# Fp16 products for three late pieces of a spectral filter, and a new order around one register load

## The chip, the cores and the metric

The kernel runs on one core of a Trainium2 chip. The metric is the device time of one execution in microseconds (us). The core has five engines with an instruction stream each: TensorE (PE, matrix products; its weight loads are shown as PEld), VectorE (DVE), ScalarE (ACT), GpSimd (POOL) and SyncE (SP). SP and POOL mostly issue DMA transfers here. Engines wait for each other through semaphores, and each works through its own stream in program order.

## The reference

Two independent computations stand side by side in one output of 2048 x 896. The left half is attention with 16 query heads of 28 dimensions and one shared key and value head; the right half is a spectral filter: a two-dimensional real FFT of a 2048 x 448 array, a product with a complex filter, and the inverse FFT.

```python
q = (x @ wq).reshape(B, S, H, Dh).transpose(0, 2, 1, 3)      # H = 16, Dh = 28
k, v = x @ wk, x @ wv
scores = einsum("bhqd,bkd->bhqk", q, k) * Dh ** -0.5
o = einsum("bhqk,bkd->bhqd", softmax(scores), v)
a = o.transpose(0, 2, 1, 3).reshape(B, S, H * Dh) @ wo

X = rfft2(x2, axes=(-2, -1)) * (w_r + 1j * w_i)
b = irfft2(X, (S, D), axes=(-2, -1))
return concatenate([a, b], axis=-1)
```

## The kernel before

The kernel has a prologue and one long attention loop.

**Prologue.** A small planner (`Plan`) takes tasks with an engine, an estimated length and dependences, and writes each engine's instruction order; TensorE's tasks keep the order in which they are added. The prologue projects queries, keys and values in split precision (L340), transforms the first pieces of the filter's input, and prepares the values for the loop: 16 transposes (L606) put the values with the positions on the partitions into one PSUM bank. They stand in two halves, `first_values` and `last_values`. `last_values` begins with `values_load`, which reads one number (`bits`) into a register of every engine. A branch on that register (L646) follows; its body, a fallback for large scores, isn't executed with these inputs. After the branch VectorE copies the turned values to SBUF (`vs`, L718), and writes the low parts of the second half of the keys (`keys_low(1)`), which two DMAs then double (`keys_twice`).

**The attention loop.** There are 4 query blocks x 4 head groups = 16 groups of 16 steps (one step is 128 key positions). A step is two score pairs (`scores`, L1258: 8 fp16 matmuls of 512 columns into two PSUM banks, then one exponential of 128 x 1024 on ScalarE, L1261) and one value group (`values`, L1277: four fp32 matmuls of 512 columns, each issued as two instructions). Six banks hold scores, three pairs in turn; nine tiles hold exponentials.

**Fillers.** Banks 6 and 7 are left. One collects the values of the group at hand, the other is free for a filler: a unit of TensorE work for something else, followed by an eviction on VectorE that frees the bank. The loop is written out ahead of time by a schedule with three clocks (`clk`): `after(when, ...)` puts VectorE's work, and DMA issues, at planned times, and `fill` puts units between steps. `owed` grows by a fixed amount per step (`EARLY`: 0.22 us until the first half of piece 7 is copied out, then 0.13 us) until the filter's last stage is open (`fb`), and from then on by what is left over the steps that are left; a unit may be placed where `owed` is above 0, outside the first step and the last two steps of a group. Unit kinds are `l` (late pieces), `w` (output projection, L1196), `z` (the filter's last stages, L1094 and L1120).

**The late pieces.** The filter's first stage runs over eight pieces q of its input. Pieces 0 to 3 are done in the prologue. Piece 4 has its features in the prologue and its points in the loop; pieces 5, 6 and 7 lie wholly in the loop. For each:

- `late_load` brings its input x (512 KB) and its point matrix w (256 KB) on SP's queue. Pieces 5 and 6 are loaded in the prologue, piece 7 behind piece 6's work.
- `late_fold` adds and subtracts mirrored rows on VectorE, in three parts.
- `late_features(q, p)`, p = 0 and 1, is TensorE's transform along the feature axis (L173, fp32, 16 matmuls of 113 columns, issued as 32 instructions), planned at 0.86 us; VectorE copies the result out (L1013).
- `late_points(q, p)` is the first transform along the position axis (L1026, fp32, 8 matmuls of 226 columns, issued as 16 instructions), planned at 0.76 us; VectorE copies it out (L1035), and SP stores it (`fft1_store`).

After piece 7, `spectrum` starts the rest of the filter on VectorE: maxima are brought together by `bounce` (write 128 x 2 numbers to DRAM, read them back to every partition, reduce), the pieces are read again across partitions (`spread`, L802, on POOL), and butterflies with the filter product in their middle follow (L817 to L939). `weight_top` takes maxima of the eight filter weight blocks ahead of that (L893), from a planned time of 24 us on. The scales of the filter's last stage come from these maxima.

## Time and profile before

| what | us |
|---|---|
| time, median of 3 runs | 579.97 |
| lowest and highest | 579.77, 580.02 |
| the profiled execution's own time | 579.57 |
| its span | 577.8 |
| TensorE busy | 571.3 |
| ScalarE busy | 513.3 |
| VectorE busy | 390.5 |
| GpSimd busy | 110.5 |

The span is the time from the first to the last instruction in the trace; the time of an execution is a little longer. A busy share is an average over stages with different limits, and matmuls overlap in their pipeline, so a TensorE that is 99% busy isn't one at its peak. In rows of instructions in order of time the columns are start, length, engine, line, operation, output and inputs, count, and in brackets the idle time before it with what ended it. Instructions that follow each other closely are merged into one row.

### The profile page before, as it was taken

The page shows a single profiled execution, that of the slowest core. Times are in us where ns is not written, and L with a number is a line of the kernel's source. Part 1 is how long each engine was busy: PE and PEld are TensorE (multiplying, and loading weights), DVE is VectorE, ACT ScalarE, POOL GpSimd, SP SyncE. Part 2 cuts the span into 40 slices and gives each one's busy share as a digit, 9 for nine tenths or more (in the row PEclk, how much of TensorE's full clock was granted, in tenths as well). Part 3 has the DMA queues.
Part 4 walks back from the last instruction along what each step waited for, and adds up shares of the span by engine and source line. Part 5 has one row for each costly group of instructions (what it writes and reads, how often), then busy time and mean ns, then how long its engine had stood idle before and what let it go on. Part 6 is the DMA issues. An engine that isn't in the chain of part 4 may idle for free.

```text
span 577.8 us, 20635 instructions
## 1 busy us (share of the span) xinstructions
PE 571.3 (99%) x8941; PEld 300.6 (52%) x8941; DVE 390.5 (68%) x747; ACT 513.3 (89%) x580; POOL 110.5 (19%) x199
## 2 busy tenths in 40 slices
PE   9999999999999999999999999999999999999997
PEld 7877454545554444444444444445455555555554
DVE  5996727955421999998998887854366743366544
ACT  4744899999999999999999999998999887899982
POOL 1023311212103012121201311123202321011110
PEclk9999999999999999999999999999999999999999
DMA  8864682625417102243301120457224341212111
GB/s 290 295 205 140 175 247 73 191 81 146 161 37 218 58 18 66 75 123 98 91 34 57 41 60 31 155 208 230 78 88 128 109 130 70 89 58 73 41 55 65
DMA packets 38502, 66.27 MB, mean 115 GB/s; under 512 B 7013, under 2 KB 28653, under 8 KB 38401
## 3 DMA queue, kind: packets, MB, share of 16 engines
q1 hardware_dynamic: 29576, 38.95, 21.1%
q0 software_dynamic: 8688, 25.76, 14.2%
q8 instruction: 70, 1.15, 0.8%
q14 instruction: 24, 0.19, 0.1%
q10 hardware_dynamic: 144, 0.23, 0.1%
HBM read 44.22 MB, written 19.97 MB: 111 GB/s over the span
## 4 chain that ended last, share of the span: by engine, by line
PE 72%; issue 7%; DVE 5%; DMA 3%; POOL 2%; ACT 0%; POOLq 0%; DVEq 0%; ACTq 0%
PE banks L1258 31%; PE banks L1277 30%; PE banks L1196 6%; PE banks L1094 2%; PE banks L1120 2%; DMA rd<-rs 1%; DMA wf<-w 1%; DVE X L817 1%; DVE X L818 1%; PE banks L1026 1%; POOL R L1164 1%; DVE X L859 1%; PE banks L173 0%; ACT yb L1208 0%; DVE w L852 0%
## 5 line engine op out<-in xcount | busy, mean ns | idle before, releaser
L1261 ACT ACTIVATE p<-banks 128x1024 f32<-128x1024 f32 x512 | 477.2, 1094 | 23.7 <-PE banks L1258 22.3
L1258 PE MATMUL banks<-qa,ka 128*32 128x512 f16 x4096 | 276.4, 379 | 0.4 <-PEq L646 0.4
L1277 PE MATMUL banks<-p,vs 128*32 128x512 f32 x2048 | 268.6, 592 | 0.0
L1258 PEld LDWEIGHTS <-ka 128*32 128x32 f16 x4096 | 129.5, 96 | 167.1 <-issue 119.1
L1277 PEld LDWEIGHTS banks<-p,vs 128*32 128x32 f32 x2048 | 69.9, 110 | 43.5 <-issue 1.7
L1156 POOL DMA_DIRECT2D sd<-qraw x15 | 10.1, 671 | 165.4 <-DVE qraw L1151 165.4
L1196 PE MATMUL banks<-woh,o 128*32 128x448 f16 x464 | 39.6, 353 | 0.1
L1164 POOL DMA_DIRECT2D R<-rd x60 | 30.8, 521 | 38.3 <-DMA rd<-rs 38.1
L1196 PEld LDWEIGHTS <-o 128*32 128x32 f16 x720 | 22.6, 97 | 27.4 <-issue 20.2
L859 DVE SCALAR_TENSOR_TENSOR X<-w,X 128x226 f32<-128x226 f32 (+2 forms) x72 | 34.1, 474 | 2.4
L1151 DVE TENSOR_SCALAR qraw<-banks,scales 128x512 f32<-128x512 f32 x15 | 11.3, 750 | 31.5 <-PE banks L1277 31.4
L1201 DVE TENSOR_SCALAR ya<-banks,scales 128x448 f32<-128x448 f32 x12 | 8.2, 683 | 27.5 <-PE banks L1196 27.5
L1127 DVE TENSOR_SCALAR w<-banks,scales 128x256 f32<-128x256 f32 x16 | 7.7, 484 | 27.3 <-PE banks L1120 27.3
L1162 POOL DMA_DIRECT2D rd<-rs x15 | 8.2, 549 | 90.1 <-DVE rs L1161 81.6
L1196 PE MATMUL banks<-wol,o 128*32 128x448 f16 x256 | 24.4, 352 | 0.0
L340 PE MATMUL banks<-xh,wqh 128*128 128x512 f32 x64 | 23.6, 399 | 0.0
L340 PE MATMUL banks<-xh,wql 128*128 128x512 f32 x64 | 23.0, 390 | 0.0
L344 ACT ACTIVATE qraw<-banks 128x512 f32<-128x512 f32 x16 | 9.3, 595 | 15.0 <-PE banks L340 15.0
L817 DVE TENSOR_TENSOR X<-X 128x904 f32<-128x904 f32 (+2 forms) x10 | 9.1, 906 | 16.1 <-DMA X<-t 16.1
L852 DVE SCALAR_TENSOR_TENSOR w<-X 128x113 f32<-128x113 f32 (+2 forms) x56 | 17.8, 356 | 0.1
L1035 DVE COPY bs<-banks 128x452 f32<-128x452 f32 x8 | 5.0, 619 | 18.6 <-PE banks L1026 18.5
L340 PE MATMUL banks<-xl,wqh 128*128 128x512 f32 x48 | 17.3, 390 | 0.0
(157 smaller groups left out, 553.1 us busy)
## 6 DMA issues: line engine op xcount, KB each, us to landing
qa<-qd SPq DMA_DIRECT2D x62, 128.0 KB
ob<-yo SPq DMA_DIRECT2D x16, 256.0 KB
t<-bs SPq DMA_DIRECT2D x16, 226.0 KB
w<-w POOLq DMA_DIRECT2D x8, 452.0 KB, 4.7
X<-t POOLq DMA_DIRECT2D x8, 452.0 KB, 7.1
wf<-w POOLq DMA_DIRECT2D x8, 452.0 KB, 4.0
x<-t POOLq DMA_DIRECT2D x8, 452.0 KB, 4.4
R<-rd POOLq DMA_DIRECT2D x60, 56.0 KB, 2.1
```

Of the source, the lines that this page charges most:

```text
L340: mm(pq[c, g], w[:, j, gs], x[:, j], start=(j == 0 and n == 0), stop=(j == 3 and n == 1))
L817: todo(226 * n, lambda: TT(both(a), both(a), both(b), op=ALU.add), at)
L852: STT(out, y, sy, x, op0=ALU.mult, op1=ALU.add if c > 0 else ALU.subtract)
L859: todo(226 * n, lambda d=d, q=q: STT(both(d), t[0].rearrange("p r n f -> p r (n f)"), q, both(a), op0=ALU.mult, op1=ALU.add))
L1094: mm(pz[r, j], fb["c2", q % 2][:, x, e, j, r], fb["fi", q % 2][:, j, f], start=(n == 0), stop=(n == 2))
L1120: mm(py[m:m + 32, k].rearrange("p (j n) -> p j n", j=4), cs3[:w, kind, f, m:m + 32], fb["z", q % 2, e][:w, x, :, 64 * r:64 * r + 64], star ...
L1151: V.tensor_scalar(o, bank[b], scale_v, None, op0=ALU.mult)
L1164: nc.gpsimd.dma_start(R[32 * i:32 * i + DH], rd[i:i + 1].to_broadcast([DH, CW]))
L1196: mm(p[r:r + 32], x[c][:, g, s][:, r:r + 32], w[:, m], start=(g == 0 and n == 0), stop=(g == NG - 1 and n == 2))
L1258: mm(bank[b + h][r], ka[:, k:k + 32], qa[c, g][:, 2 * p + h], start=True, stop=True)
L1261: nc.scalar.activation(pt[i], banks[:, b:b + 2], AF.Exp, scale=SCALE / UP / UP)
L1277: mm(bank[b][32 * i:32 * i + 32], vs[:, kc], pt[2 * st + i // 2][:, i % 2], start=(kc == 0), stop=(kc == 15))
```

## The change

Three things are changed.

1. **Fp16 products for pieces 5, 6 and 7.** Features and points of these pieces are each computed from three fp16 products (high x high, high x low, low x high) in place of one fp32 product. The constants come split into two fp16 halves, scaled by 1024. The folded input is scaled by a number taken from its maximum and split on VectorE (`late_split`, two instructions per piece), the features are split when they are copied out (two instructions in place of one), and the points' copy multiplies the scales back. The maxima of the three inputs are taken early in the loop (`late_top`) and brought together by `bounce`, now for three columns. Piece 4 stays in fp32. Piece 7's loads move to the start of the loop, in buffers of their own, and the fp16 cosines are loaded there, where the fp32 ones were.
2. **The order around the register load.** All 16 transposes of the values stand ahead of `values_load` on TensorE, with the second stage of piece 3 ahead of them; the last features of piece 4 stand behind it, and are copied out by VectorE after the branch rather than by ScalarE before it.
3. **Plan numbers.** Features are planned at 0.64 us and points at 0.58 us, points are taken in order ahead of features, the weight maxima start at a planned 14 us rather than 24, and VectorE's clock starts at 4.0 rather than 3.4.

```diff
 def late_load(q, names):
     for n in names:
-        nc.sync.dma_start(late[n, q], t["xb"][q] if n == "x" else t["fz"][:, q - L])
+        src = t["xb"][q] if n == "x" else t["fz16"][:, q - L - 1] if n == "W" else t["fz" if n == "w" else "cs16"]
+        nc.sync.dma_start(late[n, q], src)
...
-        def first_values():
+        def turn_values_all():
             turned.append(next(turn) % 6)
             turned.insert(0, view(bank[turned[0]], 16, 32))
-            turn_values(range(8))
+            turn_values(range(16))
+            small["rv"] = nc.values_load(bits.bitcast(I32)[0:1, 0:1])
...
-        tv = add(PE, 0.6, first_values, users[-6], ident_, *krow_, *fetched["v"][:7])
+        fm_task(3)
+        add(PE, 1.2, turn_values_all, users[-6], ident_, *krow_, *fetched["v"], bt_)
         users.append(None)
-        fm_task(3)
-
-        def last_values():
-            small["rv"] = nc.values_load(bits.bitcast(I32)[0:1, 0:1])
+
+        def last_features():
             pas[4, 1] = spin(2, 226)
             features(pas[4, 1], ff[4], 1)
-            turn_values(range(8, 16))
-
-        def last_evict():
-            at1[4, 1] = late["a", 4][:, 1]
-            nc.scalar.activation(at1[4, 1], pas[4, 1], AF.Copy)
         add(ACT, 1.0, lambda: keys_cast(1, ACT), krow_[0], *fetched["k1"], bt_)
-        lv = add(PE, 1.5, last_values, bt_, users[-6], *fetched["v"], *store_tasks[L - 1])
-        add(ACT, 0.5, last_evict, lv, ev_a[4, 0])
+        add(PE, 0.8, last_features, users[-6], *store_tasks[L - 1])
...
         for p in range(2):
             keys_twice(1, p)
+        nc.vector.tensor_copy(late["a", 4][:, 1], pas[4, 1])
...
-    clk = {"pe": 1.9, "dve": 3.4, "act": 2.6}
+    clk = {"pe": 1.9, "dve": 4.0, "act": 2.6}
...
+    def late_top(qs):
+        m = ap.tile([128, 8], F32, name="mt", bufs=1)
+        V.memset(m, 0.0)
+        for n, q in enumerate(qs):
+            V.tensor_reduce(m[:113, n:n + 1], late["x", q][:113], axis=AX.XY, op=ALU.max, apply_absolute_value=True)
+
+        def fix(m):
+            for n, q in enumerate(qs):
+                tops[q] = ap.tile([128, 2], F32, name=f"t{q}", bufs=1)
+                V.tensor_scalar(tops[q][:, 1:2], m[:, n:n + 1], 1.0 / ROW, None, op0=ALU.mult)
+                V.reciprocal(m[:, 4:5], m[:, n:n + 1])
+                V.tensor_scalar(tops[q][:, 0:1], m[:, 4:5], 4096.0, None, op0=ALU.mult)
+                if q in folded:
+                    after(clk["dve"], 0.75, late_split, q, 0)
+        bounce(m, fix, 3)
...
+    def late_split(q, n):
+        f, x, scale = late["f", q][:113], late["F", q][:113], tops[q][:113, 0:1]
+        if n == 0:
+            V.tensor_scalar(x[:, 0], f, scale, None, op0=ALU.mult)
+            after(clk["dve"], 1.25, late_split, q, 1)
+        else:
+            STT(x[:, 1], f, scale, x[:, 0], op0=ALU.mult, op1=ALU.subtract)
             work["l"].extend([late_features(q, 0), late_features(q, 1)])
+
+    THREE = (0, 0), (0, 1), (1, 0)
 
     def late_features(q, p):
         def go(b):
-            features(view(bank[b], 2, 226), late["f", q], p)
-            after(clk["pe"] + LAG, 0.6, out, b)
+            pa, f, c = view(bank[b], 2, 226), late["F", q], late["C", 0]
+            for e in range(2):
+                for k in range(2):
+                    for n, (x, y) in enumerate(THREE):
+                        for h in range(2):
+                            for r in range(2):
+                                r0 = 64 * h + 32 * r
+                                mm(pa[r0:r0 + 32, e, 113 * k:113 * k + 113], f[:113, x, 2 * r + k, 2 * p + e, h],
+                                   c[:113, 2 * r + k, y], start=(n == 0), stop=(n == 2))
+            after(clk["pe"] + LAG, 1.3, out, b)
             if q < 7 and p:
-                after(clk["pe"] + (1.8 if q == 5 else 5.0), 1.22, late_fold, q + 1)
+                after(clk["pe"] + 1.8, 1.22, late_fold, q + 1)
 
         def out(b):
-            V.tensor_copy(late["a", q][:, p], view(bank[b], 2, 226))
+            a, pa = late["A", q][:, p], view(bank[b], 2, 226)
+            k = 2.0 ** -17
+            V.tensor_scalar(a[:, 0], pa, k, None, op0=ALU.mult)
+            STT(a[:, 1], pa, k, a[:, 0], op0=ALU.mult, op1=ALU.subtract)
             free[b] = clk["dve"] + 0.1
-            after(clk["dve"] + 0.2, 0.0, work["l"].appendleft, late_points(q, p))
-        return 0.86, go
+            after(clk["dve"] + 0.2, 0.0, late_ready, q, p)
+        return 0.64, go
...
             for h in range(2):
-                for e in range(2):
-                    for m in (0, 32):
-                        mm(pb[64 * e + m:64 * e + m + 32, h], late["w", q][:, h, 2 * p + e, m:m + 32], late["a", q][:, p, e],
-                           start=True, stop=True)
+                for n, (x, y) in enumerate(THREE if q > L else ((0, 0),)):
+                    for e in range(2):
+                        for m in (0, 32):
+                            w, a = ((late["W", q][:, h, x], late["A", q][:, p, y]) if q > L else
+                                    (late["w", q][:, h], late["a", q][:, p]))
+                            mm(pb[64 * e + m:64 * e + m + 32, h], w[:, 2 * p + e, m:m + 32], a[:, e],
+                               start=(n == 0), stop=(n == 2 or q == L))
             after(clk["pe"] + LAG, 0.6, out, b)
-            if q == 6 and p:
-                late_load(7, "w")
...
-    after(24.0, 0.0, weight_top, 0)
+    after(14.0, 0.0, weight_top, 0)
     work["l"].extend([late_points(4, 0), late_points(4, 1)])
-    after(3.0, 1.22, late_fold, 5)
-    total = 12 * 2.09 + 32 * 0.67 + 6 * 0.86 + 8 * 0.76
+    late_load(0, "C")
+    for n, size in (("x", 1024), ("W", 512)):
+        shaped(n, 7, ap.tile([128, size], F32, name=n + "7", bufs=1))
+        late_load(7, n)
+    after(6.0, 3.4, late_top, (5, 6, 7))
+    after(6.1, 1.22, late_fold, 5)
+    total = 12 * 2.09 + 32 * 0.67 + 6 * (0.64 + 0.58) + 2 * 0.76
```

`bounce` takes the number of columns, and both of its uses with different widths share one landing tile (`mw`, one buffer).

More of the change, by code (lines that the diff above doesn't have):

```diff
@@ L165, with features @@
     at1 = {}
-    def features(pa, f, p):
-        for e in range(2):
+    def features(pa, f, p, es=(0, 1)):
+        for e in es:
             for k in range(2):
@@ L1000, in late_fold @@
         else:
[L1001 to L1002 removed]
+            folded.add(q)
+            if q in tops:
+                after(clk["dve"], 0.75, late_split, q, 0)
+    def late_split(q, n):
[5 more added lines that the diff above has]
+            STT(x[:, 1], f, scale, x[:, 0], op0=ALU.mult, op1=ALU.subtract)
```

64 lines of the change are left out of this document (41 added, 23 removed).

## The prediction

> **What bounds the kernel now.** I read the page's busy shares first, then TensorE's instructions in order of time inside the attention loop, then ScalarE's exponentials by stretches.
>
> ```profile
> PE 571.3 (99%) x8941; PEld 300.6 (52%) x8941; DVE 390.5 (68%) x747; ACT 513.3 (89%) x580; POOL 110.5 (19%) x199
> ```
>
> TensorE and ScalarE are both near full, so the shares alone don't say which of the two sets the end. The pace of a loop step does. A step is two score pairs and one value group (L1277 x8); the starts of successive value groups, in a stretch right after a filler and in one without any:
>
> ```profile
> 171.45 1.04 PE L1277 MATMUL banks<-p,vs 128*32 128x512 f32 x8
> ...
> 173.17 1.05 PE L1277 MATMUL banks<-p,vs 128*32 128x512 f32 x8
> ...
> 192.29 1.04 PE L1277 MATMUL banks<-p,vs 128*32 128x512 f32 x8
> ...
> 194.13 1.04 PE L1277 MATMUL banks<-p,vs 128*32 128x512 f32 x8
> ```
>
> 173.17 - 171.45 = 1.72 us is TensorE's own pace (0.86 for the scores, 0.86 for the values), 194.13 - 192.29 = 1.84 us is ScalarE's pace, at which TensorE has 0.11 to 0.12 us of every step free. Any filler (late pieces, filter stages, output projection) beyond 0.11 us per step therefore lengthens the loop one for one, and any stretch with less filler loses TensorE time. The exponentials show where this happens:
>
> ```profile
> 62.70:169.65 106.95, 103.87 (x112) 1.00 0.47 140
> 169.65:229.60 59.95, 59.71 (x66) 1.00 0.31 94
> 229.60:389.50 159.90, 159.12 (x173) 1.00 0.28 88
> 389.50:562.40 172.90, 154.49 (x163) 1.00 0.29 96
> ```
>
> ```profile
> 220.95 0.37 PE L1196 MATMUL banks<-woh,o 128*32 128x448 f16 x4
> ```
>
> Columns: stretch, length, busy time with count, clock, DMA share, GB/s. From 62 to 167 the late pieces hold ScalarE up (0.95 us per exponential), in the next stretch (0.91 us) ScalarE becomes the bound and TensorE waits once its backlog is worked off, and from the first projection filler at 220.95 on TensorE is the bound to the end, most of all from 389.5 (1.06 us per exponential). The granted clock is 1.00 in every row. So the end is TensorE's work plus TensorE's idle time, and that idle time lies in the first 160 us of the loop. A saving of TensorE work counts in full unless it comes back as waiting there.
>
> **Fp16 products.** Each late unit's TensorE price is the distance to the next group's start:
>
> ```profile
> 77.45 0.96 PE L173 MATMUL banks<-spol,spoh 113*32 113x113 f32 x32
> 78.23 0.62 PE L1258 MATMUL banks<-qa,ka 128*32 128x512 f16 x8
> ...
> 166.38 0.95 PE L1026 MATMUL banks<-spol 128*32 128x226 f32 x16
> 167.15 1.03 PE L1258 MATMUL banks<-qa,ka 128*32 128x512 f16 x13
> ...
> 402.97 0.86 PE L1094 MATMUL banks<-fi,c 128*32 128x128 f16 x48
> 403.64 0.62 PE L1258 MATMUL banks<-qa,ka 128*32 128x512 f16 x8
> ...
> 422.63 0.84 PE L1120 MATMUL banks<-z,cs 113*32 113x256 f16 x24
> 423.29 1.05 PE L1258 MATMUL banks<-qa,ka 128*32 128x512 f16 x16
> ```
>
> A features unit costs 0.78 us, a points unit 0.77 us in fp32. The new units have the same shape as two that are in this trace: 48 fp16 matmuls with four column groups side by side and 128 columns take 0.67 us (twelve rounds of 56 ns), 24 with 256 columns take 0.66 us (six rounds of 110 ns). The line through these is 1.6 ns + 0.424 ns per column. New features: twelve rounds of 113 columns, 12 x 49.5 = 0.59 us; new points: six rounds of 226 columns, 6 x 97.4 = 0.58 us. Bounds for the features: 0.59, and 0.67 if 48 instruction pairs can't go faster than in the 128-column row. Six units of each: 6 x 0.19 + 6 x 0.19 = 2.3 us less, 1.8 at the other bound. I take 2.2. Piece 4 stays fp32.
>
> One page speaks against this. The Trainium skill ("TensorE: Matmul & The Clock Gate", section "Wait — 56ns, not 53.3ns?") says that matmuls never start closer together than about 25 ns, however small they are. By that, 48 products would take 1.2 us and the change would lose on every features unit. The row above disagrees: 48 products in 0.67 us is 14 ns each, with column groups side by side.
>
> **The order of late units.** Step 0's values start here:
>
> ```profile
> 65.17 1.04 PE L1277 MATMUL banks<-p,vs 128*32 128x512 f32 x8
> ```
>
> Units are let in at 0.22 us of filler per step, and at 0.13 once the first half of piece 7 is copied out (the two numbers of EARLY), not in the last two steps or the first step of a group of 16. This rule gives today's places (the last points unit at 166.38 is step 53). With units of 0.64 and 0.58 in the plan, and piece 5's features not before its scale is known (planned about 27 us into the loop, step 13, and 65.17 + 13 x 1.83 = 89.0 us), I count the last points unit to step 49 or 50, near 158 us (166.38 less 3.5 steps and the 2.2 us saved): 3 or 4 steps sooner. From there to the projection fillers at about step 86 TensorE follows ScalarE, so 3.5 steps more at 0.11: **+0.4 us**. Between piece 4 (its second unit comes at step 4) and step 13 there is no filler any more. Its backlog lasts some seven steps, then two to six steps idle 0.11 each: **+0.3 us**, with 0 and 0.7 as ends.
>
> **VectorE, queues and loads.**
>
> ```profile
> L1081 DVE SCALAR_TENSOR_TENSOR c<-x,scales,c 128x904 f16<-128x904 f32 x8 | 9.3, 1159 | 0.7
> L893 DVE TENSOR_REDUCE peaks<-w 128x1 f32<-128x904 f32 x8 | 8.7, 1087 | 0.0
> L1080 DVE TENSOR_SCALAR c<-x,scales 128x904 f16<-128x904 f32 x8 | 5.5, 690 | 9.5 <-PE banks L1094 9.5
> ```
>
> ```profile
> 60.00:90.00 30.00, 29.56 (x472) 14.56 (x470) 14.70 (x27) 27.70 (x32) 5.88 (x11) 1.00 0.74 215
> 90.00:120.00 30.00, 30.00 (x472) 14.75 (x468) 27.79 (x46) 28.92 (x32) 6.53 (x12) 1.00 0.44 132
> 120.00:170.00 50.00, 50.00 (x776) 26.51 (x772) 22.50 (x39) 48.68 (x54) 8.57 (x16) 1.00 0.34 101
> ```
>
> Scaled to 1024 columns: three maxima x 1.23 = 3.7 us, three splits x (0.78 + 1.31) = 6.3, six second evictions x 0.6 = 3.6 (452 columns, between the two rates above), the copy of piece 4 0.6, some ten tiny scale operations 1.7: 16 us more for VectorE. It has 15.3 us free before 90 and 27.5 after 120 (30 - 14.70, 50 - 22.50), 2.2 between. The eight weight maxima move 10 us forward, part of them out of the full stretch. So I cost this at nothing; without that cover each microsecond by which an eviction comes late is a microsecond of TensorE. The loads of piece 7 (512 and 256 KB) leave their places in SP's queue behind piece 6 and go, with the fp16 cosines (226 KB), to the loop's start. They stand behind the key copies, which the scores need, and ahead of the next query block and the new maximum's round trip; DMA is 74% busy there. On POOL the first weight load now stands ahead of one projection load and the X loads, and waits for the scratch buffers; X's first reader stands far behind in VectorE's program. New waits: VectorE waits for piece 7's landing at the third maximum, with the fold of piece 5 and the maxima of the values behind it, for which TensorE waits first at step 13; SP waits, since both round trips now share one landing tile, with the second's fetch until the first is reduced, and the following query block's stores behind it are wanted a group later. I cost these at nothing too, and price the round trip as a rival. The filter's transforms should start some 10 us sooner; since TensorE is the bound from 220.95 on, that is worth nothing.
>
> **The prologue.**
>
> ```profile
> 57.88 0.65 PE L606 MATMUL banks<-ident,kf 32*128 32x32 f32 x8
> 58.46 0.99 PE L183 MATMUL banks<-a,fw 64*64 64x226 f32 x16
> 59.87 0.98 PE L173 MATMUL banks<-spol,f 113*32 113x113 f32 x32 [0.41 <-issue]
> 60.78 0.68 PE L606 MATMUL banks<-ident,kf 32*128 32x32 f32 x8
> 61.87 0.99 PE L1258 MATMUL banks<-qa,ka 128*32 128x512 f16 x12 [0.40 <-PEq L646]
> ```
>
> TensorE executes the same matmuls before and after. It idles 0.41 us at the register load and 0.40 us at the branch. The change puts 16 transposes (2 x 0.58 us, 58.46 - 57.88) rather than 0.99 us of stage-two products ahead of the load, and 0.98 us of features rather than 0.68 us of transposes ahead of the branch; if the sequencer runs ahead of the array, more of each gap is hidden. Ends: -0.8 (both gaps gone), +0.4 (the load fully exposed). I take **-0.2**. The values' copy on VectorE comes about 1 us sooner, and the removed ScalarE copy ended before the first exponential's scores were there; neither is on the path, since the first value product waits for exponentials.
>
> **Sum**: -2.2 + 0.4 + 0.3 - 0.2 = -1.7 us. The profiled execution took 579.57 us (577.8 span and 1.8 around it), 0.4 below the median of 579.97. So 577.9 by the profile, **578.3** by the median. A second count, from ScalarE's side: 10.8 us of filler over 53 steps with 0.11 free leave 5.0 us exposed; 1.5 + 7.1 us over 49.5 steps leave 3.2. That is 1.8 less before the prologue's 0.2.
>
> **Rivals.** (1) *Eaten gain.* Features at 0.67 (saving 1.8), 0.7 idle before step 13, nothing from the prologue: -1.8 + 0.4 + 0.7 = -0.7, 579.3 us. For it: ScalarE is nearly full up to 220.95. (2) *Gaps gone.* Both prologue gaps close and no idle comes back early: -2.2 - 0.8 + 0.2 = -2.8, 577.2 us. (3) *Slower: the scale comes late.* Piece 5's features stand in TensorE's program at step 13 whether or not the scale has arrived, and scores and values queue behind them. The present round trip of this kind:
>
> ```profile
> 74.03 0.34 SPq L911 DMA_DIRECT2D md<-m  x1
> 85.74 0.34 SPq L913 DMA_DIRECT2D mw<-md  x1
> 89.05 0.44 DVE L916 TENSOR_REDUCE m<-mw 128x2 f32<-128x256 f32 x1 [2.23 <-DMA mw<-md]
> ```
>
> It takes 15.0 us under the load traffic. If piece 7 lands only at 74 us, the maximum is out at 75.5, back at 90.5, and after 0.7 + 1.5 + 2.1 us of reduce, scales and split the features start at 94.8 instead of 89: 5.8 us. ScalarE has two finished score pairs in hand (1.8 us), so 4.0 us are lost: 579.97 - 1.7 + 4.0 = 582.3. It decides when the split ends after about 93.7 (loss over 4.7 - 1.8 = 2.9, slower by 0.2%). Against it: the maximum should leave VectorE soon after 70 (three maxima behind the first late eviction), ahead of the X loads that the old trip stood behind. (4) *Pair floor.* The fp32 features row holds 32 matmuls in 0.78 us, 24.4 ns each. If that is the least spacing and not the length of fp32 streaming, 48 products take 1.17 us (+0.39 a unit) and 24 take 0.59 (-0.18), 6 x 0.21 = +1.3, with the +0.7 and -0.2 above 581.8 us. The 14 ns row speaks against it. The page cited above states a floor of this size.
>
> **Chances.** About 0.2% (1.2 us) is what a measurement of this kernel can tell from no change. Forecast (577.6 to 578.8) 0.42; gaps gone 0.16; eaten gain 0.28; late scale 0.11; pair floor 0.03. Faster 0.58, same 0.28, slower 0.14. The range 576.8 to 580.4 takes in the first three cases with their ends and leaves the two slower ones out.
>
> **What would show it.** Features units should stand 0.59 to 0.67 us and points units 0.58 us ahead of the next group; the last points unit near 158; the value steps at 1.83 from there to about 219; no TensorE gap at the first features of piece 5; the gaps before the last features and the first scores below 0.41 and 0.40. Wrong if TensorE waits at late units for VectorE, or if the time from the first projection filler to the end is no longer TensorE's work alone.

## The result and the profile after

The changed kernel takes **584.6 us** (median of 6 executions, 581.84 to 585.4), the kernel before 579.87 in the same sitting: ratio 1.0079, 95% interval 1.0058 to 1.0099. It is slower by 4.7 us, outside the predicted range of 576.8 to 580.4. The profiled execution took 584.45 us (span 582.7). The changed kernel's lines have other numbers than those shown above: scores L1317, values L1336, exponentials L1320, late features L1052, late points L1084, group eviction L1210, landing of a round trip L922, its store and fetch L917 and L919.

The page's busy shares of the kernel after:

```profile
PE 571.4 (98%) x9085; PEld 303.2 (52%) x9085; DVE 406.2 (70%) x775; ACT 512.7 (88%) x579; POOL 110.0 (19%) x199
```

TensorE is busy as long as before (571.3), VectorE 15.7 us longer (16 were predicted). The span is 4.9 us longer, so the loss is idle time, or work at a lower clock, which busy time doesn't tell apart.

To find when it came, I use VectorE's eviction of a finished value group (its timeline: start, duration, instruction, idle before it and what ended that). Where it waits for TensorE, its start marks the end of a group of 16 steps. The first of these is called group 0's here; the seventh (the expectations call it group 7's), before and then after:

```profile
275.38 0.75 DVE L1151 TENSOR_SCALAR qraw<-banks,scales 128x512 f32<-128x512 f32 x1 [1.37 <-PE banks L1277]
```

```profile
279.35 0.75 DVE L1210 TENSOR_SCALAR qraw<-banks,scales 128x512 f32<-128x512 f32 x1 [1.40 <-PE banks L1336]
```

4.0 of the 4.9 us are there before 280, behind the last late piece. At the third eviction, which waits for TensorE in both kernels too, it is 5.0 us (162.23 against 157.25). TensorE's timeline after, around the first features unit of piece 5:

```profile
96.18 1.04 PE L1336 MATMUL banks<-p,vs 128*32 128x512 f32 x8
100.12 0.80 PE L1052 MATMUL banks<-spol,spoh 113*32 113x113 f16 x48 [2.90 <-DVE qraw L1210]
100.73 2.22 PE L1317 MATMUL banks<-qa,ka 128*32 128x512 f16 x24
102.70 1.96 PE L1336 MATMUL banks<-p,vs 128*32 128x512 f32 x8
...
107.33 0.77 PE L1084 MATMUL banks<-spol 128*32 128x226 f16 x24
107.92 1.52 PE L1317 MATMUL banks<-qa,ka 128*32 128x512 f16 x24
```

The units are as small as predicted: features 100.73 - 100.12 = 0.61 us, points 107.92 - 107.33 = 0.59. But ahead of this unit TensorE waits 2.90 us for VectorE's group eviction, whose bank the unit is to use; and behind the wait a value group takes 1.70 us (102.70 to 104.40) where it took 0.86. The same time by stretches (length, then busy time of TensorE, its weight load, VectorE, ScalarE and GpSimd, granted clock, DMA share, GB/s):

```profile
100.00:101.00 1.00, 0.88 (x56) 0.78 (x59) 0.96 (x3) 0.00 (x0) 0.59 (x1) 1.00 0.38 131
101.00:102.00 1.00, 1.00 (x20) 0.54 (x16) 1.00 (x2) 0.54 (x1) 0.00 (x0) 0.66 0.53 152
102.00:103.00 1.00, 1.00 (x16) 0.49 (x11) 0.97 (x3) 1.00 (x2) 0.00 (x0) 0.50 0.62 187
103.00:104.00 1.00, 1.00 (x8) 0.20 (x4) 0.35 (x1) 1.00 (x2) 0.00 (x0) 0.50 0.25 73
104.00:105.00 1.00, 1.00 (x39) 0.59 (x34) 0.00 (x0) 0.31 (x1) 0.26 (x1) 0.63 0.48 137
105.00:106.00 1.00, 1.00 (x47) 0.68 (x36) 0.58 (x1) 0.09 (x1) 1.00 (x3) 1.00 0.05 2
```

The granted clock falls to one half for 3.4 us: 0.34 + 0.50 + 0.50 + 0.37 = 1.7 us of TensorE lost. The Trainium skill ("TensorE: Matmul & The Clock Gate", section "What's actually happening") says that the array runs at half its clock after an idle window of about 3.4 us, until a busy window of that length; the trace agrees on the half and on its length, and shows that 2.9 us of idle time can be enough.

Why was the eviction late? Before the change it stood here, and waited for TensorE:

```profile
94.75 0.75 DVE L1151 TENSOR_SCALAR qraw<-banks,scales 128x512 f32<-128x512 f32 x1 [1.54 <-PE banks L1277]
```

VectorE's timeline after, cut to the chain:

```profile
73.09 1.22 DVE L1009 TENSOR_REDUCE mt<-x 113x1 f32<-113x1024 f32 x1 [3.94 <-DMA x<-xb]
...
78.06 0.16 DVE L789 TENSOR_TENSOR m<-m 128x1 f32<-128x1 f32 x1
...
84.91 0.75 DVE L922 TENSOR_REDUCE mt<-mw 128x3 f32<-128x384 f32 x1 [2.13 <-DMA mw<-md]
...
93.43 0.42 DVE L922 TENSOR_REDUCE m<-mw 128x2 f32<-128x256 f32 x1 [4.69 <-DMA mw<-md]
...
95.39 1.28 DVE L1038 SCALAR_TENSOR_TENSOR spoh<-spoh,t 113x1024 f16<-113x1024 f32 x1
96.59 0.45 DVE L774 TENSOR_SCALAR woh<-wo,scales 128x448 f16<-128x448 f32 x1
...
99.33 0.74 DVE L1210 TENSOR_SCALAR qraw<-banks,scales 128x512 f32<-128x512 f32 x1
```

`mt` is the new maximum of the late pieces, `m` the old one of the values and output weights, whose scale the group eviction multiplies by. The values' maximum is out at 78.2 instead of 72.3, its landing is reduced at 93.43 instead of 89.05, and between its scales and the eviction now stand 3.9 us (95.39 to 99.33) of split, weight split and query work, of which the kernel before had the weight split there and the query work behind the eviction. SP's queue shows the other half:

```profile
76.30 0.38 SPq L917 DMA_DIRECT2D md<-mt  x1
78.55 0.34 SPq L919 DMA_DIRECT2D mw<-md  x1
78.93 0.42 SPq L917 DMA_DIRECT2D md<-m  x1
88.68 0.32 SPq L919 DMA_DIRECT2D mw<-md  x1
```

Both trips are a store and a fetch on one queue, in the order store, fetch, store, fetch: the values' store stands behind the first trip's fetch, which waits for that trip's store. In this execution that held it up by no more than 0.7 us (78.22 to 78.93). The values' trip itself took no longer than before (14.5 us against 15.0); what made it late here is that their maximum left VectorE 5.9 us later.

So the first reading, up to the seventh eviction: fp16 -2.1 (6 x 0.17 + 6 x 0.18), prologue -0.2 (first values at 64.96 instead of 65.17), wait +2.9, half clock +1.7, a second wait of 0.72 us at piece 6's split: +3.0 of the 4.0. Two more terms stand in TensorE's timeline after:

```profile
83.35 1.04 PE L1336 MATMUL banks<-p,vs 128*32 128x512 f32 x8
...
85.18 1.04 PE L1336 MATMUL banks<-p,vs 128*32 128x512 f32 x8
...
227.39 0.37 PE L1255 MATMUL banks<-woh,o 128*32 128x448 f16 x4 [1.19 <-DMA o<-lows]
```

Without fillers, nine steps from 80 to 96 us come at ScalarE's pace of 1.83 us, where those of the kernel before, with its fillers between them, come at 1.72 but for one: +1.0. The first projection filler waits 1.19 us for a transfer; before, it waited for nothing. Against these, from 170 to 225 us only 12 steps come at ScalarE's pace instead of 21, about -0.9. The terms add up to +4.3, where 4.0 were measured.

### The profile page after: what moved, and what is told of

The parts are those of the page before. It is cut to its first block, busy times and chain, and to the rows that moved or that the text cites. A ratio compares the mean times of both kernels' runs of the same rounds, so it can differ in the third digit from the quotient of the medians.

```text
span 582.7 us, 20949 instructions
## 1 busy us (share of the span) xinstructions
PE 571.4 (98%) x9085; PEld 303.2 (52%) x9085; DVE 406.2 (70%) x775; ACT 512.7 (88%) x579; POOL 110.0 (19%) x199
## 4 chain that ended last, share of the span: by engine, by line
PE 77%; DMA 5%; DVE 4%; issue 1%; ACT 1%; SPq 0%; POOL 0%; DVEq 0%; ACTq 0%; POOLq 0%
PE banks L1317 34%; PE banks L1336 33%; PE banks L1255 6%; DMA mw<-md 2%; PE banks L1153 2%; PE banks L1179 2%; DMA qd<-qh 1%; DVE peaks L899 1%; DMA sd<-qraw 1%; DMA wo<-wo 0%; PE banks L1052 0%; DVE spoh L1038 0%; PE banks L1084 0%; DMA md<-mt 0%; ACT yb L1267 0%
## 5 line engine op out<-in xcount | busy, mean ns | idle before, releaser
L1320 ACT ACTIVATE p<-banks 128x1024 f32<-128x1024 f32 x512 | 477.0, 1101 | 29.7 <-PE banks L1317 29.2
L1317 PE MATMUL banks<-qa,ka 128*32 128x512 f16 x4096 | 277.1, 380 | 0.6 <-PEq L651 0.4
L1336 PE MATMUL banks<-p,vs 128*32 128x512 f32 x2048 | 268.9, 594 | 0.0
L1317 PEld LDWEIGHTS <-ka 128*32 128x32 f16 x4096 | 129.6, 96 | 168.8 <-issue 125.3
L1336 PEld LDWEIGHTS banks<-p,vs 128*32 128x32 f32 x2048 | 70.1, 110 | 43.0 <-issue 2.0
L1255 PEld LDWEIGHTS <-o 128*32 128x32 f16 x720 | 23.8, 97 | 26.0 <-issue 19.6
L1210 DVE TENSOR_SCALAR qraw<-banks,scales 128x512 f32<-128x512 f32 x15 | 11.2, 749 | 20.4 <-PE banks L1336 20.4
L939 DVE TENSOR_TENSOR w<-X,wf 128x904 f32<-128x904 f32 x16 | 17.0, 1097 | 0.2
```

Source lines behind the costliest of these rows:

```text
L939: TT(u[r], both(s), wt[k][:, r:r + 1].to_broadcast([128, 2, 452]), op=ALU.mult)
L1210: V.tensor_scalar(o, bank[b], scale_v, None, op0=ALU.mult)
L1255: mm(p[r:r + 32], x[c][:, g, s][:, r:r + 32], w[:, m], start=(g == 0 and n == 0), stop=(g == NG - 1 and n == 2))
L1317: mm(bank[b + h][r], ka[:, k:k + 32], qa[c, g][:, 2 * p + h], start=True, stop=True)
L1320: nc.scalar.activation(pt[i], banks[:, b:b + 2], AF.Exp, scale=SCALE / UP / UP)
L1336: mm(bank[b][32 * i:32 * i + 32], vs[:, kc], pt[2 * st + i // 2][:, i % 2], start=(kc == 0), stop=(kc == 15))
```

## The experiments

Eighteen kernels ran. Each batch had its own executions of the kernel before (medians 579.62 to 579.84). "Median" is that of the kernel named; single waits are those of its profiled execution.

### What the first batch tells apart

**The prologue alone**, on the kernel before.

> The kernel before with the prologue's part of the change alone: all sixteen turned value blocks and the register load ahead of the last features of piece 4, whose second half VectorE copies out behind the branch instead of ScalarE ahead of it. No fp16 products, no moved loads. My theory (the loss lies in the loop, at the first features of piece 5): the two gaps shrink as in the changed kernel, first value group about 0.2 us sooner, 579.4 to 579.9 where the kernel before has 579.9; the granted clock stays 1.00 in 90 to 110 us. Rival (the prologue itself costs): 581 or more. By neither theory is there an idle stretch of TensorE over 1 us near 100 us.

578.84 us (578.56 to 579.34), ratio 0.9985 (0.9976 to 0.9994). TensorE's timeline:

```profile
59.92 0.98 PE L173 MATMUL banks<-spol,f 113*32 113x113 f32 x32
61.33 1.05 PE L1253 MATMUL banks<-qa,ka 128*32 128x512 f16 x16 [0.42 <-PEq L640]
```

The gap at the register load is gone, the one at the branch stays at 0.42. The first scores start at 61.33 instead of 61.87, the seventh eviction at 274.4 instead of 275.4. This part is worth 0.8 us (by the interval 0.3 to 1.4), more than the 0.2 of the prediction and of the range expected here. One trace can't size it: in the profiled executions of the other kernels that have this prologue the first scores start anywhere from 61.25 to 62.15.

**The features held back**: one gate in the plan.

```diff
-            work["l"].extend([late_features(q, 0), late_features(q, 1)])
+            after(max(clk["dve"], 42.0), 0.0, work["l"].extend, [late_features(q, 0), late_features(q, 1)])
```

> The changed kernel with one line different: the features units of pieces 5 to 7 are not put before 42 us of the plan, so the first of them stands behind step 21's work in TensorE's program and not behind step 18's. The same instructions on VectorE, the same loads and waits, the same splits. My theory (TensorE waits 2.9 us at that unit for a bank which VectorE frees late, since VectorE waits in order for the second round trip; behind that idle time the granted clock is halved for some 3.4 us): the second trip's reduce is as late as before (93 us), but no stall over 0.7 us at the unit, no clock under 0.9 between 98 and 108 us, so about 3.0 + 1.7 us less than the changed kernel's 584.6: 579 to 581. Rival A (VectorE's 16 us of added work or the fp16 products themselves cost): 583 or more, with the stall gone. Rival B (the second late trip will hold up something else just behind, such as the next query block): a new wait of over 2 us in 95 to 110 us, and 582 to 584.

581.88 us (580.66 to 584.15). At step 21 the unit starts without a wait, as expected; but the next one, in TensorE's timeline, waits and is slow:

```profile
110.98 1.33 PE L1052 MATMUL banks<-spol,spoh 113*32 113x113 f16 x48 [3.12 <-DVE spol L1062]
```

VectorE evicts the first unit late because it stood still for a load of output weights. That load's timeline on GpSimd's queue, and then VectorE's:

```profile
100.12 0.60 POOL L1215 DMA_DIRECT2D sd<-qraw  x1 [20.53 <-DVE qraw L1210]
103.10 0.56 POOL L1216 DMA_DIRECT2D rs<-sd  x1 [2.38 <-DMA sd<-qraw]
103.65 0.54 POOL L771 DMA_DIRECT2D wo<-wo  x1
```

```profile
106.61 0.45 DVE L774 TENSOR_SCALAR woh<-wo,scales 128x448 f16<-128x448 f32 x1 [4.69 <-DMA wo<-wo]
```

The load stands behind two transfers of group 0's own, which wait for its late eviction (99.08 here). In the kernel before the same load left at 99.87, and VectorE didn't wait for it. So rival B had the mechanism: what the late trip delays holds up something else just behind, and the wait moved to the next bank. Its time (582 to 584) is missed by 0.1 us. The first theory, that one wait of TensorE is the whole of it, falls.

**Without the wait for piece 7**, and **with its loads late too**.

```diff
-    after(6.0, 3.4, late_top, (5, 6, 7))
+    after(6.0, 2.3, late_top, (5, 6))
+    after(44.0, 1.2, late_top, (7,))
...
-        late_load(7, n)
+        after(26.0, 0.0, late_load, 7, n)
```

> The changed kernel with the maximum of piece 7 taken out of the first round trip and sent in a trip of its own 38 us later; its 0.74 MB of loads stay at the loop's start, and a gate keeps the first features of piece 5 behind step 18's values. My theory: VectorE no longer waits 3.9 us for piece 7's landing, the maxima of the values leave at about 74 instead of 78 us, the second trip is back by 89 to 90 instead of 93.4, the stall at the first features falls from 2.9 to under 0.7 us and the clock stays over 0.9: 579 to 581.5. Rival (the trips are late by the load traffic alone, and the wait for piece 7 only hid behind it): the second reduce still ends its wait after 92.5, the stall is 2 us or more, 583 to 585.

> As the run before, and the two loads of piece 7 (512 and 256 KB) are issued 26 us into the loop, not at its start. My theory: the query block's reload lands in 3 to 4 us instead of 8, the first trip is back by 82 instead of 84.9, the second by 86 to 89; no stall over 0.5 us, the clock 1.00 throughout: 578.3 to 580.5, equal to the run before or up to 1 us better. If the traffic alone is the cause (rival), this run is 580 and the run before 583 or more.

The first 584.78 (583.2 to 586.2), the second 580.0 (577.74 to 582.51, ratio 1.0011, 1.0000 to 1.0023). My theory is refuted, and its rival's two times hold: with no wait for piece 7 the stall grew to 4.8 us. SP's queue in that run:

```profile
75.35 1.13 SPq L917 DMA_DIRECT2D md<-mt  x1
87.34 0.34 SPq L919 DMA_DIRECT2D mw<-md  x1
87.73 0.42 SPq L917 DMA_DIRECT2D md<-m  x1
```

The values' maximum was ready at 72.8, and its store left at 87.73, behind the other trip's fetch. With the loads late it left at 79.0, was reduced at 91.0, and TensorE didn't wait at the unit (but 0.86 us at 115.58). So taking VectorE's wait for piece 7 away gains nothing by itself: the other trip, behind the loads, then holds up the values' store instead, by 15 us.

### Traffic, order and VectorE's timetable

**Weight loads later** (the changed kernel, `weight_top` from 24 us), **both later** (that and piece 7's loads and trip), and **traffic alone** (two loads, 768 KB in all, added to the kernel before).

> The changed kernel with the chain of weight maxima, each with a 452 KB load, started at 24 us of the plan as before the change and not at 14; piece 7's loads stay at the loop's start and its maximum in the first round trip; a gate keeps the first features of piece 5 behind step 18's values. What is left of the added load traffic up to 90 us is piece 7's 0.77 MB and the cosines. Theory A (the second round trip is late by the bytes that the change puts in front of it at the loop's start, 0.99 MB on SP's queue): the first weight load comes after the trip in any case, the second trip is back at 92 to 94 us as in the changed kernel, group 0's eviction at 99 to 100, the stall 2.5 us or more, 583.5 to 585.5. Theory B (the weight loads made ten us sooner collide with the trip): back by 90, stall under 0.7 us, 579.5 to 581.5.

> Both: piece 7's loads 26 us into the loop with a round trip of their own, and the weight maxima from 24 us of the plan; the first features of piece 5 behind step 18's values. Theory A: like the run with piece 7's loads late alone (580.0 median, 577.7 the fastest), second trip back by 91, no stall at the first features; with fewer loads between 95 and 110 us fewer late evictions, so 577.5 to 579.5 and a narrower spread. Theory B: better than that run by 1 us or more. Rival (the fp16 products and their VectorE work give nothing back): 579 or more with no stall and a clock of 1.00.

> The kernel before with nothing of the change but its traffic: 512 KB of piece 7's values and 256 KB of its factors are loaded once more at the loop's start, into tiles that nothing reads. Theory A: the query block's reload and the round trip are later by about 3 us (0.77 MB at the 220 to 270 GB/s of that stretch), the reduce that ended at 89.5 us comes at 92 to 94; group 0's eviction, wanted at 94, is then late by 1 to 3 us, but the late unit that follows it stands at step 17 and needs its bank at 96, so a stall of 0 to 2 us: 579.7 to 582.5. Rival (the loads cost only together with the fp16 pieces' own waits): 579.4 to 579.9 and the reduce within 1 us of where it was.

Medians 584.03 (581.32 to 585.17), 583.36 (580.79 to 586.02), 579.36 (578.97 to 579.96). The first is as theory A says: the time hardly changes. The second misses: the values' reduce came at 93.8, 2.8 us later than in the run with piece 7 late alone, though less was loaded; I have no cause for that beyond the trips' own spread. The third shows VectorE's rows of the old order under the new traffic:

```profile
90.65 0.44 DVE L916 TENSOR_REDUCE m<-mw 128x2 f32<-128x256 f32 x1 [3.02 <-DMA mw<-md]
...
95.56 0.75 DVE L1151 TENSOR_SCALAR qraw<-banks,scales 128x512 f32<-128x512 f32 x1 [0.75 <-PE banks L1277]
```

The reduce comes 1.6 us later (90.65 against 89.05), half of it because in this execution the loop starts 0.8 us later (62.68 against 61.87), and the eviction still waits for TensorE. Theory A's times (92 to 94, and 579.7 or more) are missed, and the kernel's time is the rival's: the loads cost nothing by themselves. The old timetable had some slack (1.54 us of waiting for TensorE at 94.75), and the change spent it.

The run with the weight loads later also shows a stall without the half clock: its unit waited 2.71 us, and the stretch behind it reads

```profile
100.00:105.00 5.00, 4.73 (x132) 2.99 (x135) 3.58 (x7) 3.40 (x4) 0.77 (x2) 1.00 0.45 141
```

That execution took 581.32, the three others of this kernel 583.67 to 585.17. Of the six executions of the changed kernel the one with a mean clock of 0.999 took 581.84, the five at 0.996 to 0.997 took 584.45 or more.

**The values' trip first**: the late pieces' maxima behind those of the values (`late_top` at 12 us), their reduce behind the eviction; then the same with piece 7 late, and with the weight maxima late too.

> The changed kernel with all its traffic as it is (piece 7's loads at the loop's start, the weight loads early) and only the order of the two round trips turned round: VectorE takes the maxima of the values ahead of those of the late pieces, so that the trip that group 0's eviction needs goes first in SP's queue, and the reduce of the late pieces' trip stands behind that eviction. The first features of piece 5 come at step 22, the last points unit at step 53. Theory C (what costs is that the two trips go one behind the other in SP's queue, store, fetch, store, fetch, and that the one that the eviction needs goes second): the values' reduce ends at 88 to 91.5 us, as in the kernel before (89.5), group 0's eviction by 96.5, no wait of TensorE for it, the clock 1.00 up to 100; 578 to 580 if nothing else is late. Theory A (the added traffic alone): the reduce comes at 92.5 or later and the eviction after 97.5; 581 or more.

> As the run before, with piece 7's loads 26 us into the loop and its maximum in a trip of its own. First features of piece 5 at step 21, last points unit at step 57. Theory C: the values' reduce by 90, no stall anywhere over 0.7 us, 577 to 578.8; that is the fp16 saving of 2 us and the prologue's 0.8, and 0.3 to 0.8 us less than the run before. If the fp16 products save less than the 2 us that their units show, 578.8 or more with no stall.

> As the run before, and the chain of weight maxima from 24 us of the plan. First features of piece 5 at step 20, last points unit at step 55. Theory C: within 0.5 us of the run before, 577 to 578.8. If the weight loads made early collide with the trips, 0.5 us or more better than it.

580.2 (578.92 to 582.61), 582.49 (579.73 to 584.65), 583.18 (580.48 to 585.36). All three take the first wait away, and in all three TensorE waits later, at 109 to 118 us. In the first of them, VectorE's landing and then TensorE's wait:

```profile
92.04 0.42 DVE L922 TENSOR_REDUCE m<-mw 128x2 f32<-128x256 f32 x1 [11.76 <-DMA mw<-md]
```

```profile
111.56 0.76 PE L1084 MATMUL banks<-spol 128*32 128x226 f16 x24 [2.31 <-DVE spol L1062]
```

The landing lies between the bounds of the two theories (91.5 and 92.5). Behind it VectorE waits 3.52 us for output weights (107.19), as in the gated kernel, and evicts late. In the two others TensorE waits 1.51 us at 116.48 and 1.39 us at 116.30, while ScalarE stands idle too; the traces don't show for what. The order of the trips is a cause of the first wait, and not of the loss as a whole. Theory C's times were missed by 0.2, 3.7 and 4.4 us.

**Relief for VectorE**: output weights 22 us and the first transform's maxima 12 us later, on the gated kernel and on the one with the values' trip first.

```diff
-        at = 24.0 + 6 * g if g < NG else 60.0 + 6 * g
+        at = 46.0 + 6 * g if g < NG else 60.0 + 6 * g
...
-    after(34.0, 0.0, first_points)
+    after(46.0, 0.0, first_points)
```

> The changed kernel with three numbers different: the late features not before 42 us of the plan (first ones at step 21), and out of VectorE's full stretch from 95 to 125 us two things that nothing needs before 165: the loads and splits of the output weights begin 22 us later, the maxima of the first transform 12 us later. Trips, loads of piece 7 and splits as in the changed kernel. Theory D (the loss is VectorE alone: its in-order waits for transfers and its full program up to 125 us hold back the evictions of group 0 and of the late units, and TensorE waits for their banks): the wait of 4.7 us for output weights at 102 is gone, no wait of TensorE over 0.7 us between 90 and 130 us, clock 1.00, 577.3 to 579. Theory A (transfers ahead of the trips): the trip is late as before, group 0's eviction at 98 to 99, but no late unit wants its bank; the same. If the fp16 products are worth less than their units show: no stall and 579.3 or more.

> The run with the values' trip first and piece 7 late, with the same relief of VectorE: output weights 22 us and first transform's maxima 12 us later. First features of piece 5 at step 20, last points unit at step 61. Theory D: VectorE evicts the first features unit within 2 us of its end, no wait of TensorE over 0.5 us before 220 us, 576.5 to 578.3, the least of all kernels here, and a spread under 1.5 us. If the unit for unit saving of 2.2 us is eaten by ScalarE's pace instead: 578.5 to 579.5 with no stall.

586.67 (583.35 to 589.59) and 591.54 (588.81 to 593.24): the largest misses. In the first, TensorE waits nowhere over 0.3 us from 64 to 200 us, so that half of theory D held; the work that I took for harmless came due later, with a wait of 1.44 us for a transfer at 222.76 and this one:

```profile
417.86 0.85 PE L1153 MATMUL banks<-fi,c 128*32 128x128 f16 x48 [3.06 <-DVE ya L1260]
```

This is the fastest execution of the six (583.35); no trace shows what the others lost. In the second kernel theory D fails before 220 already: TensorE waits 1.11, 2.10 and 2.19 us for VectorE at 126.02, 141.34 and 162.63.

### Products, trip and volume apart

Of the first three of these four, the first and the third leave out the scales of the late pieces, the first and the second the low halves.

> The changed kernel with TensorE's work as it is and VectorE's added work and waits taken out: the scales of the late pieces are the constant 1 (no maxima, no round trip for them, no wait for piece 7), and the low halves of features and stage-one results are set to zero by GpSimd once or in the split's place, not worked out by VectorE. All added loads stay where the change puts them. First features of piece 5 at step 18, last points unit at step 53. Theory D (the products save what their units show, and everything lost is VectorE's): no wait of TensorE over 0.5 us between 62 and 220, group 7's eviction, 275.4 in the kernel before and 279.4 in the changed one, at 272.5 to 273.8, and 576.5 to 577.8 in all. Theory A (the transfers): the values' trip is late still, group 0's eviction after 96.5, 578.5 or more. If the products themselves gain nothing: 578.5 to 579.5 with no wait.

> As the run before, but with the maxima of the late pieces, the wait for piece 7 and the round trip as in the changed kernel; only the low halves are left out (9 of VectorE's ops, 7.6 us). If it is the trip and its place ahead of the values' trip that costs: group 0's eviction at 97.5 or later, a wait of 1.5 to 3 us at the first features, and 579.5 to 583.5. If it is VectorE's volume of work: 577 to 578.5.

> The other way round: scales constant, no maxima and no trip of the late pieces, but all low halves worked out by VectorE as in the changed kernel. If it is the trip that costs: no stall before 105, 577 to 578.8. If it is the volume of work: stalls of 1 to 3 us between 100 and 125 behind late evictions, 579 to 582.

> The run with piece 7's loads and trip late (580.0 median, 577.7 to 582.5), with the first features of piece 5 two steps later, at step 20. If the slow ones among its executions were those in which the values' trip came 3 us later than in the profiled one, two steps (3.7 us) cover that: median 577.5 to 578.8 and a spread under 2 us. If it was anything behind 105 us: 579.5 to 581 again.

Medians 579.17 (577.53 to 584.32), 581.47 (580.37 to 582.43), 580.89 (578.37 to 584.8), 584.26 (581.56 to 585.25). The products alone, in VectorE's timeline of the profiled execution (577.53, the fastest of twelve):

```profile
273.26 0.75 DVE L1209 TENSOR_SCALAR qraw<-banks,scales 128x512 f32<-128x512 f32 x1 [1.00 <-PE banks L1335]
```

That is 2.1 us ahead of the kernel before and 1.1 ahead of the prologue alone, and the list of TensorE's waits from 62 to 575 us is empty. So in this execution the products pay, by about what the prediction left of them (2.2 less 0.7). By the median they don't show: 579.17 misses theory D's 576.5 to 577.8, is 0.3 above the prologue alone, and can't be told from the kernel before (ratio 0.9993, 0.9974 to 1.0012). What the slower executions lost, up to 584.32, stands in no trace. The first features' wait, with the trip alone and then with the volume alone:

```profile
100.04 0.80 PE L1052 MATMUL banks<-spol,spoh 113*32 113x113 f16 x48 [2.39 <-DVE qraw L1209]
```

```profile
98.32 0.79 PE L1052 MATMUL banks<-spol,spoh 113*32 113x113 f16 x48 [0.89 <-DVE qraw L1210]
```

By medians the trip costs 2.3 us and the volume 1.7 over the products alone. The trip's cost came as expected (eviction at 99.2, time in the range). The volume's is less sure: its interval overlaps that of the products alone, and the stalls expected from 100 to 125 us didn't come; beside the 0.89 at 98.32 there is one of 1.53 at 221.71, for the fifth eviction. The fourth run was to show that two steps more of distance suffice; it was 4.3 us worse than the same kernel two steps earlier, with a wait of 3.77 us at its second features unit, behind VectorE's wait of 5.50 us for output weights (108.31).

### The same work in another place

Piece 5 stays fp32 with its old places, only pieces 6 and 7 are fp16, and none of the new loads stands ahead of the values' trip, none of the new maxima and splits ahead of group 0's eviction:

```diff
-    after(6.0, 3.4, late_top, (5, 6, 7))
-    after(6.1, 1.22, late_fold, 5)
...
+    after(16.0, 0.0, late_load, 7, "x")
+    after(28.0, 0.0, late_load, 0, "C")
+    after(28.5, 0.0, late_load, 7, "W")
+    after(36.0, 2.3, late_top, (6, 7))
+    after(3.0, 1.22, late_fold, 5)
...
```

The second of the two has 48.0 in place of 36.0.

> The change for pieces 6 and 7 alone: piece 5 stays fp32 with its features at steps 7 and 17 as in the kernel before, the late pieces' maxima and trip stand behind group 0's eviction on VectorE, piece 7's and the cosines' loads behind the values' trip on SP, the weight maxima from 24 us; the prologue of the change. First fp16 features at step 28, last points unit at step 51. Theory D (VectorE's added work and waits cost where it is full, 95 to 125 us, and the trip where it goes ahead of the values' trip): the values' reduce by 90, group 0's eviction at 94, no wait of TensorE over 0.5 us before 110; four units save 0.19 each in place of six pairs, 1.5 us, with the prologue's 0.8: 577.0 to 578.3 if the splits at 110 to 118 hold nothing up, 578.3 to 580 if they do. If the products save nothing in the loop: 578.8, as the prologue alone.

> As the run before, with the late pieces' trip 12 us later: the splits fall behind 125 us, where VectorE has a third of its time free, the first fp16 features stand at step 35, the last points unit at step 56. Theory D: no wait of TensorE over 0.5 us before 220 us and a spread under 1.5 us, 577.0 to 578.3, at or under the run before. If the filter's later start costs at the end (last points three steps later than in the kernel before): up to 1.5 us more, 578.3 to 579.5.

The first takes **577.11 us** (576.96 to 577.49), ratio 0.9959 (0.9946 to 0.9972): 2.5 us faster than the kernel before, 7.5 faster than the changed one, and inside the range expected. It is 1.7 faster than the prologue alone, where the eight fp16 units were expected to bring 1.5: this run, which differs from that one in loads and plan numbers too, is the one whose median speaks for the products. Its VectorE timeline:

```profile
86.58 0.43 DVE L921 TENSOR_REDUCE m<-mw 128x2 f32<-128x256 f32 x1 [0.29 <-DMA mw<-md]
...
94.21 0.75 DVE L1218 TENSOR_SCALAR qraw<-banks,scales 128x512 f32<-128x512 f32 x1 [3.49 <-PE banks L1344]
...
272.43 0.75 DVE L1218 TENSOR_SCALAR qraw<-banks,scales 128x512 f32<-128x512 f32 x1 [1.40 <-PE banks L1344]
```

VectorE waits only 0.29 us for the landing, the eviction waits 3.5 us for TensorE and not the other way, and the list of TensorE's waits from 62 to 575 us is empty. VectorE is busy 400.5 us in all, 10 more than before, and that is hidden. Three things differ from the changed kernel at once here: less VectorE work, the trips in the old order, and piece 5's fp32 units as fillers at steps 7 and 17. The run doesn't tell them apart.

The second takes 580.37 (578.89 to 582.51), over both of the ranges expected. Its profiled execution is the slowest (582.51). It is as good up to 170 us (third eviction at 155.1 against 155.9), 0.9 us behind at the seventh, and loses the rest in the filter, first in VectorE's timeline and then in TensorE's:

```profile
408.32 0.25 DVE L1228 RECIPROCAL rs<-rs 128x16 f32<-128x16 f32 x1 [4.51 <-DMA rs<-sd]
```

```profile
409.90 0.37 PE L1263 MATMUL banks<-woh,o 128*32 128x448 f16 x4 [2.85 <-DVE z L1170]
```

Again VectorE waits in order for a small transfer, and TensorE for the bank that VectorE would empty next. Behind this wait too the granted clock falls, to 0.50 to 0.70 from 410 to 414.

## Why the prediction was wrong

**The step that failed** is the pair of sentences on VectorE, queues and loads, "So I cost this at nothing" and, of the new waits, "I cost these at nothing too". Both the work and the waits cost: 1.7 (the less sure of the two) and 2.3 us over the products alone, and together, in the changed kernel, a wait of 2.9 us with 1.7 us of half clock behind it. The prediction named VectorE's wait for piece 7 and that the maxima of the values stand behind it; it didn't follow these on to group 0's eviction, whose bank TensorE wanted at 97.22 and got at 100.12. The sign that it gave for being wrong, TensorE waiting at late units for VectorE, came true. Free time summed over a stretch, of 15.3 and 27.5 us, was no cover. Up to the eviction of group 0 VectorE, which runs its program in order, waited 2.2 us for transfers before the change and 10.8 after it (3.94 + 2.13 + 4.69). The work behind these waits slid into the stretch from 95 to 125, where little was free, and where TensorE wants a bank at every late unit.

**The rival "the scale comes late"** (582.3, chance 0.11) had the kind of event and its side, and the wrong trip. It followed piece 5's split, which did end after its deciding point of 93.7, at 96.7; but the unit stood at step 18, not 13, and by then waited not for its split but for the bank of group 0's eviction, which hangs on the second trip. That the two trips go one behind the other on SP's queue was in the diff and in the text ("both round trips share one landing tile"), but its effect on the old trip was put at nothing, and only the new trip got a price.

**The order of late units** was miscounted: piece 5's first features at step 18 instead of 13, the last points unit at step 51, 168.2 us, instead of 49 to 50 near 158. So the idle time before it was 1.0 us (nine steps at ScalarE's pace) and not 0.3, above the end of 0.7 that was given.

**Fp16 products**: right in size, 2.1 us against 2.2: 0.61 and 0.59 us for a unit against the 0.59 and 0.58 that were taken. In the fastest execution of the products alone 1.1 us of it is left over the prologue at the seventh eviction. The pair floor falls: 48 products in 0.61 us are 13 ns each.

**The prologue**: the direction right, the size low, -0.8 against -0.2, at the end of the range that was given (-0.8). That end stood for both gaps gone, but only the one at the load (0.41) went and the one at the branch stayed (0.42); so half of the gain comes from something that the prediction doesn't have, and what it is stays open. In the changed kernel's trace the first scores were at 61.70 and not at 61.33, which lies within the scatter of this start.

**"The filter's transforms should start some 10 us sooner ... that is worth nothing"**: not tested in that direction. In the other, in the two kernels where they started later, the traces show TensorE waiting about 3 us for VectorE at 410 to 418 us.

**The clock** was read as 1.00 in every row and left out of the sum. It has a price as soon as a wait lasts, here 1.7 us.

## What to carry to other kernels

Don't set added work on an in-order engine against its free time in a stretch: look what each free stretch waits for, and what on the bounding engine waits for the next instruction behind it. Follow a late eviction on, too: here the next load of weights stood behind it on GpSimd's queue, and VectorE's next wait behind that load. Where a small round trip is added beside an old one on the same queue, ask first whether the old one's store now stands behind the new one's fetch. Work that is off the path should stand behind the last instruction that the bound waits for and ahead of the next: one trip 12 us later, with the splits and units behind it, cost 3.3 us (577.11 against 580.37).

## What was not expected of the hardware

Waits of TensorE of 2.85, 2.90, 3.12, 3.77 and 4.79 us were each followed by a granted clock of one half for some 3 us or more (in the last from 100 to 106 us, the wait's own end included); waits of 2.31, 2.39, 2.69, 2.71 and, once, 3.06 us were not. In the second relief kernel one of 2.16 us at 569.14, with three of 0.19 to 0.43 close behind it, was. So a wait near 3 us costs itself and then, in some executions, about 1.7 us more: that fits part of the spread from 581.8 to 585.4 us in the changed kernel. Two kernels whose traces show no wait of TensorE over 0.2 us in the loop, the prologue alone and the one with two fp16 pieces, spread by 0.8 and 0.5 us; a third, the products alone, spreads by 6.8 us, so the traced execution doesn't speak for all.

A store of 1 KB and a fetch of it, spread to all partitions, took 15.0 us (74.03 to 89.05) in the kernel before, 14.5 us (78.93 to 93.43) in the changed one, and 9.0 us (87.73 to 96.68) where it left some 10 us later. How much of it is time behind other transfers isn't shown. The two runs with piece 7 late, which differ in when the weight loads start, had the values' landing at 91.0 and 93.8; the first of them with its features two steps later, the same work up to there, had it at 94.1. So one trip scatters by some 3 us between executions.
